# The constants' load moved behind the first loads of a_re and a_im

## The chip, the cores and the metric

The kernel runs on one core of a Trainium2 chip. The core has five engines that work side by side, each through its own list of instructions in order: PE (TensorE, matrix products), ACT (ScalarE, functions), DVE (VectorE), POOL (GpSimd) and SP (SyncE, which here only issues transfers). Sixteen DMA engines move the data; SP and ACT can both issue transfers, each through a queue of its own, and both queues are worked off by the same sixteen engines. The metric is the device time of one execution in microseconds (us), the median of several runs.

## The reference, cut to what matters

A gated linear recurrence with complex gates over 4 batches, 8 heads, 768 positions and 48 channels, followed by a feed-forward block over the 3072 rows of its output:

```
mag = sqrt(a_re^2 + a_im^2); scale = min(mag, 0.999) / (mag + 1e-6)
a = (a_re + i a_im) * scale
for t in range(768):  S = a[t] * S + outer(k[t], v[t]);  y[t] = q[t] @ real(S)
h = y @ w_in;  solu = h * softmax(h);  ln = layernorm(solu) * g_ln;  out = ln @ w_out
```

The kernel does not step through t. It takes the logarithm of the gates' size and their angle, sums both along a chunk of 128 positions by a product with a triangular matrix of ones on PE, and turns the sums back into factors on q and k. With these, a chunk is a masked product of q and k, times v, plus what the state carries over. So nothing of a chunk can reach PE before a_re and a_im of that chunk have gone through ACT and DVE, and PE's first product needs the triangular matrix, one of the constants.

## The kernel before

The work is cut into 6 stretches of 128 positions times 4 batches, 24 chunks in all. Two chunks (a pair of batches) form a group: 12 groups share the loads and the preparation of the gates. The feed-forward block follows chunk by chunk. The weights arrive as 64-bit numbers and are converted on the core in 7 pieces during the first groups.

The order on every engine is written out by hand: the string `ORDER` (from L516) names some 1,200 steps as `name:index`, and the loop at the end of `whole` calls them in that order. Each step appends its instructions to the lists of the engines that it uses, SP's included, so the order in `ORDER` is also the order of the issues of transfers. A name without a step, as `init:0`, does nothing.

The first steps, in the order of the string: `load_aia`, `load_ara`, `load_arb`, `load_aib` (`load_one`, L702 to L707) load a_im and a_re of group 0, half by half, 192 KB each; only group 0 is loaded and prepared in halves, a and b. `inverse` (L823) has ACT take the logarithm of a_re (L824, f_lr) and its reciprocal (L825, f_x). `ratio` has DVE multiply a_im by it (L830) and a_re by it (L831). Then come `sure`, `tangent`, `square`, `secant`, `size`, `eps`, `lnm`, alternating between ACT and DVE, until f_lr holds the logarithm of the gates' size. `total` (L881) multiplies it by the triangular matrix on PE into f_L: the first work of PE, 8 products for each half. `decay` and `grow` take the exponentials, `last` sends the last row to f_rows (L900), `turn_ends` reads f_rows on PE into f_tot.

Between these, SP issues further loads: `load_q`, `fetch:5` and `fetch:1` (a piece of w_out as two transfers, and a piece of w_in, into f_raw, L746), `load_v`, `load_k`, `fetch:0` (a piece of w_in into f_w_mix), and, behind `last`, a_im and a_re of group 1, further weight pieces and `load_vr` (L715, f_vr: four transfers of v in another row order, read with f_v by the product f_y, L1087). `up` (L1128) is the feed-forward block's first product, f_h.

The constants f_mats are five matrices of 128 x 128 (unit matrix, triangular matrices, ones), 320 KB, kept as data of the program. One transfer brings them in, issued by ACT ahead of its first step:

```
1279  to_exp()
1280  nc.scalar.dma_start(out=mats, in_=nc.inline_tensor(fast_constants(), ...
```

`to_exp` loads ACT's table of logarithm and exponential. f_mats is read by PE in `total`, and later in `phase`, the transposes and the masks.

The transfers issued by SP and ACT together use eight completion semaphores. Each transfer is given one of them when the program is built, and SP waits before each issue until the last transfer with the same semaphore has landed. In the program before, f_mats has the third place in this count, behind the first halves of a_im and a_re; f_q has the sixth.

Of the kernel before, what the change touches and what calls it, by code (L numbers as in the profile page):

```python
# [516 lines left out]
init:0 load_aia:0 load_ara:0 inversea:0 load_arb:0 ratioa:0 load_aib:0 surea:0 load_q:0 tangenta:0 fetch:5 fetch:1  # L517
inverseb:0 squarea:0 ratiob:0 secanta:0 sureb:0 sizea:0 load_v:0 tangentb:0 epsa:0 load_k:0 lnma:0 squareb:0 secantb:0
fourthb:0 sizeb:0 total0:0 epsb:0 fourtha:0 raised:5 lnmb:0 decay0:0 grow0:0 total1:0 grow1:0 decay1:0 fetch:0 trig:0
anglea:0 convert:5 phase0:0 last:0 raised:1 qs0:0 angleb:0 convert:1 phase1:0 nearest0:0 part0:0 turn_ends:0  # L520
nearest1:0 ks0:0 ks1:0 sina:0 cosa:0 load_ai:1 qs1:0 part1:0 q2:0 tot:0 sinb:0 k2:0 cosb:0 exp:0 qt1:0 load_ar:1 qT1:0
raised:0 q2:1 kt1:0 k2:1 convert:0 kT1:0 inverse:1 ratio:1 kt0:0 qt0:0 qT0:0 kT0:0 fetch:2 score1:0 fetch:6 qt0:1
qT0:1 load_vr:0 score0:0 qt1:1 sure:1 raised:2 load_q:1 mask0:0 values:0 tangent:1 kt1:1 fetch:3 square:1 secant:1
turned_x:0 convert:2 qT1:1 up0:0 fetch:4 raised:6 size:1 eps:1 convert:6 lnm:1 fourth:1 onward:0 up1:0 gain:0 total1:1
load_k:1 kT1:1 raised:3 exp0:0 grow1:1 total0:1 decay0:1 grow0:1 carry:1 convert:3 solu0:0 decay1:1 trig:1 angle:1
kt0:1 phase1:1 ks1:1 qs0:1 kT0:1 add:1 phase0:1 ks0:1 score1:1 raised:4 nearest0:1 score0:1 nearest1:1 convert:4
part0:1 carry:0 part1:1 mean:0 mean:3 mean:7 add:0 sin:1 cos:1 mask0:1 load_q:2 q2:2 k2:2 mean:1 zt0:0 exp:1 load_ar:2
mean:4 mean:2 inverse:2 values:1 mean:5 kqb:2 turned_x:1 load_ai:2 ratio:2 mean:6 zT0:0 meansum:0 again:5 last:1
centre:3 centre:7 up1:1 sure:2 tangent:2 load_v:1 kqt0:2 square:2 zt1:0 centre:1 centre:2 secant:2 centre:0 centre:4
size:2 centre:6 eps:2 centre:5 up0:1 k2:3 turn_ends:1 qs1:1 score1:2 lnm:2 onward:1 centred:0 load_vr:1 score0:2 tot:1  # L530
down0:0 total0:2 zT1:0 total1:2 load_k:2 q2:3 exp0:1 fourth:2 mask0:2 down1:0 solu0:1 decay0:2 grow0:2 grow1:2
load_ar:3 decay1:2 kqb:3 trig:2 mixed:1 zt0:1 kqt0:3 last:2 values:2 angle:2 spread:0 zT0:1 on:2 phase1:2 ks1:2 norm:0
qs0:2 turned_x:2 phase0:2 carry:2 load_ai:3 nearest1:2 nearest0:2 up0:2 part1:2 part0:2 sin:2 add:2 cos:2 ks0:2 k2:4
q2:4 centred:1 exp:2 zt1:1 zT1:1 inverse:3 scale:0 up1:2 kqb:4 score1:3 score0:3 down0:1 mask0:3 ratio:3 exp0:2
turn_ends:2 spread:1 sure:3 solu0:2 load_q:3 values:3 tangent:3 load_v:2 down1:1 square:3 tot:2 turned_x:3 secant:3
size:3 load_k:3 carry:3 qs1:2 up0:3 kqt0:4 eps:3 norm:1 up1:3 k2:5 onward:2 zt1:2 lnm:3 lh:3 zt0:2 exp0:3 q2:5 scale:1
zT0:2 zT1:2 fourth:3 score1:4 ll:3 score0:4 mixed:0 total0:3 load_vr:2 total1:3 down0:2 kqb:5 down1:2 solu0:3 decay0:3
grow0:3 grow1:3 decay1:3 mask0:4 add:3 centred:2 trig:3 blocks:3 values:4 angle:3 on:3 xh:3 kqt0:5 store:1 store:0
spread:2 xl:3 last:3 phase1:3 turned_x:4 phase0:3 ks0:3 ks1:3 qs0:3 nearest0:3 score1:5 load_ar:4 centred:3 score0:5
nearest1:3 carry:4 load_ai:4 norm:2 part0:3 up0:4 part1:3 sin:3 cos:3 up1:4 mask0:5 turn_ends:3 exp:3 add:4 scale:2  # L540
k2:6 q2:6 away:3 inverse:4 values:5 exp0:4 kqb:6 ratio:4 down0:3 load_q:4 solu0:4 spread:3 turned_x:5 sure:4 load_v:3
tangent:4 qs1:3 down1:3 carry:5 kqt0:6 square:4 blocks:4 secant:4 size:4 onward:3 up0:5 away:4 eps:4 k2:7 norm:3 up1:5
q2:7 lnm:4 lh:4 tot:3 fourth:4 score1:6 ll:4 score0:6 exp0:5 total0:4 load_vr:3 load_k:4 kqb:7 total1:4 kqt0:7 solu0:5
scale:3 decay0:4 grow0:4 grow1:4 decay1:4 mask0:6 add:5 down0:4 trig:4 down1:4 centred:5 values:6 angle:4 on:4 xh:4
centred:4 qs0:4 xl:4 spread:4 last:4 store:2 phase1:4 turned_x:6 phase0:4 ks1:4 nearest0:4 ks0:4 nearest1:4 blocks:5
score1:7 carry:6 load_ai:5 part0:4 load_ar:5 part1:4 norm:4 score0:7 up0:6 sin:4 add:6 turn_ends:4 cos:4 exp:4 scale:4
away:5 store:3 inverse:5 mask0:7 up1:6 k2:8 q2:8 kqb:8 values:7 spread:5 exp0:6 ratio:5 down0:5 sure:5 load_q:5
solu0:6 turned_x:7 load_v:4 tangent:5 down1:5 square:5 qs1:4 kqt0:8 blocks:6 secant:5 onward:4 carry:7 up0:7 norm:5
size:5 eps:5 q2:9 k2:9 away:6 load_vr:4 lnm:5 up1:7 load_k:5 lh:5 fourth:5 scale:5 exp0:7 score1:8 ll:5 score0:8
total0:5 tot:4 kqb:9 total1:5 down0:6 kqt0:9 solu0:7 grow1:5 decay1:5 mask0:8 decay0:5 grow0:5 trig:5 down1:6 add:7  # L550
centred:7 blocks:7 values:8 angle:5 on:5 inspect:5 xh:5 centred:6 xl:5 spread:6 phase1:5 last:5 qs0:5 store:4
turned_x:8 phase0:5 ks1:5 load_ar:6 nearest1:5 nearest0:5 ks0:5 carry:8 load_ai:6 score0:9 score1:9 part1:5 part0:5
mask0:9 up1:8 sin:5 norm:6 up0:8 cos:5 add:8 turn_ends:5 scale:6 exp:5 inverse:6 store:5 k2:10 q2:10 values:9 kqb:10
ratio:6 exp0:8 solu0:8 away:7 turned_x:9 onward:5 down0:7 load_q:6 sure:6 down1:7 load_v:5 spread:7 tangent:6 square:6
blocks:8 qs1:5 kqt0:10 carry:9 secant:6 fourth:6 up0:9 norm:7 size:6 k2:11 away:8 eps:6 lnm:6 tot:5 load_vr:5 up1:9
q2:11 lh:6 scale:7 exp0:9 load_k:6 score0:10 score1:10 ll:6 total0:6 kqb:11 total1:6 down0:8 kqt0:11 solu0:9 grow1:6
decay1:6 mask0:10 decay0:6 grow0:6 trig:6 down1:8 add:9 centred:9 blocks:9 angle:6 values:10 on:6 xh:6 centred:8
store:6 xl:6 qs0:6 spread:8 last:6 phase1:6 turned_x:10 phase0:6 nearest0:6 ks1:6 nearest1:6 score1:11 carry:10
load_ai:7 score0:11 ks0:6 load_ar:7 away:9 part0:6 part1:6 cos:6 up0:10 sin:6 norm:8 mask0:11 up1:10 turn_ends:6
scale:8 exp:6 add:10 inverse:7 spread:9 store:7 values:11 k2:12 q2:12 kqb:12 ratio:7 exp0:10 down0:9 onward:6 solu0:10  # L560
load_q:7 turned_x:11 sure:7 down1:9 tangent:7 qs1:6 carry:11 load_v:6 kqt0:12 square:7 blocks:10 up0:11 secant:7
size:7 norm:9 eps:7 k2:13 away:10 load_vr:6 scale:9 lnm:7 tot:6 up1:11 q2:13 lh:7 fourth:7 exp0:11 score1:12 load_k:7
ll:7 score0:12 total0:7 kqb:13 total1:7 down0:10 centred:10 kqt0:13 solu0:11 grow1:7 decay1:7 mask0:12 decay0:7
grow0:7 trig:7 down1:10 add:11 blocks:11 angle:7 values:12 on:7 xh:7 last:7 store:8 spread:10 centred:11 qs0:7 xl:7
ks0:7 phase1:7 turned_x:12 phase0:7 nearest1:7 ks1:7 nearest0:7 score0:13 score1:13 part1:7 part0:7 mask0:13 sin:7
load_ar:8 away:11 carry:12 load_ai:8 up0:12 cos:7 add:12 norm:10 turn_ends:7 scale:10 exp:7 store:9 up1:12 k2:14 q2:14
inverse:8 values:13 kqb:14 ratio:8 exp0:12 solu0:12 down0:11 load_q:8 turned_x:13 sure:8 down1:11 load_v:7 tangent:8
carry:13 qs1:7 spread:11 kqt0:14 square:8 blocks:12 secant:8 norm:11 size:8 onward:7 k2:15 tot:7 eps:8 away:12 lnm:8
load_vr:7 fourth:8 up0:13 lh:8 load_k:8 up1:13 q2:15 score1:14 score0:14 ll:8 scale:11 total0:8 kqb:15 total1:8
exp0:13 decay0:8 grow0:8 centred:12 mask0:14 grow1:8 decay1:8 down0:12 kqt0:15 solu0:13 trig:8 down1:12 add:13  # L570
centred:13 blocks:13 angle:8 values:14 on:8 xh:8 store:10 spread:12 xl:8 last:8 phase1:8 turned_x:14 phase0:8 ks0:8
score0:15 qs0:8 nearest0:8 score1:15 ks1:8 nearest1:8 part0:8 carry:14 load_ai:9 part1:8 sin:8 norm:12 mask0:15 cos:8
add:14 load_ar:9 up1:14 turn_ends:8 exp:8 up0:14 away:13 k2:16 q2:16 scale:12 inverse:9 store:11 values:15 kqb:16
ratio:9 exp0:14 spread:13 load_v:8 solu0:14 turned_x:15 sure:9 down0:13 load_q:9 down1:13 tangent:9 blocks:14 square:9
# [38 lines left out]
def whole(ctx, tc, flag, q, k, v, a_re, a_im, moe_w_in, moe_w_out, moe_g_ln, out):  # L613
# [663 lines left out]


    to_exp()
    nc.scalar.dma_start(out=mats, in_=nc.inline_tensor(fast_constants(), name="f_mats_np").ap().rearrange("p (n t) -> p n t", n=5))  # L1280
    nc.vector.memset(unit, 1.0)
    nc.vector.memset(quarter, -0.5 * math.pi)
    nc.vector.memset(small, math.log(1e-6))
# [90 lines left out]
```

## Time and profile before

| | |
|---|---|
| median of 3 runs | 415.65 us (415.19 to 415.83) |
| the profiled execution | 415.1 us, of which 413.1 are its span |
| granted clock of PE | 0.996 of full speed |
| DMA engines | 74.17 MB, 180 GB/s over the span; queue of SP 72.64 MB, queue of ACT 0.43 MB |
| f_ai, first half | issued 0.72, landing 3.9 us after |
| f_ar, first half | issued 1.23, landing 4.3 us after |
| f_mats | issued 0.75 by ACT, landing 3.1 us after |
| PE's first product (f_L) | 13.27 |

Times count from the start of the span. "SPq" and "ACTq" are issues of transfers; the time beside one is how long the engine stood in the issue, not how long the transfer took. What a transfer took is the time "to landing", from its issue to the moment its data are announced. The chain of waits is followed back from the last instruction of the run: each step is what released the next one, so that its early part says what the start of the run waited for. An engine that waits while another is busy costs nothing unless it stands in that chain.

### The profile page before, as it was taken

How to read it: one execution, taken by the hardware profiler on the slowest of the kernel's cores; microseconds unless marked ns; L12 is line 12 of the kernel's file. 1: busy time of each engine (PE TensorE's matmuls, PEld its weight loads, DVE VectorE, ACT ScalarE, POOL GpSimd, SP SyncE). 2: the span in 40 equal slices, each digit the busy share in tenths (PEclk: the TensorE clock that was granted, in tenths of full speed). 3: DMA queues.
4: the chain of work that ended last, by engine and by line, in shares of the span. 5: the costliest groups of instructions: out<-in, count | busy, mean ns of one | idle time of the engine just before them, and what ended most of it. 6: DMA issues, size and time to landing. Idle time of an engine off the chain costs nothing.

```text
span 413.1 us, 15874 instructions
## 1 busy us (share of the span) xinstructions
PE 379.1 (92%) x6968; PEld 202.7 (49%) x6968; DVE 337.0 (82%) x414; ACT 299.0 (72%) x487; POOL 64.5 (16%) x140
## 2 busy tenths in 40 slices
PE   0368779999999999999999999999999999999995
PEld 0025334455645554654554554555645656546543
DVE  3798999779799899898899889988988988855530
ACT  4997977977887777887877976877976967721332
POOL 3000000112112112112122112112112122101111
PEclk9999999999999999999999999999999999999998
DMA  9995947695877778877787877967759768797551
GB/s 216 286 280 153 222 101 171 159 211 128 207 165 170 167 177 180 182 157 167 179 175 165 207 163 160 206 157 172 163 138 215 158 155 206 232 208 187 171 216 49
DMA packets 167741, 74.17 MB, mean 180 GB/s; under 512 B 142576, under 2 KB 156016, under 8 KB 166896
## 3 DMA queue, kind: packets, MB, share of 16 engines
q1 hardware_dynamic: 167376, 72.64, 74.7%
q8 instruction: 57, 0.93, 0.9%
q10 hardware_dynamic: 288, 0.43, 0.4%
q14 instruction: 20, 0.16, 0.1%
HBM read 38.87 MB, written 4.72 MB: 106 GB/s over the span
## 4 chain that ended last, share of the span: by engine, by line
PE 81%; ACT 8%; DVE 5%; DMA 2%; issue 1%; SPq 1%; DVEq 0%; ACTq 0%
PE f_h L1128 28%; PE f_o L1193 27%; PE f_y L1087 9%; PE f_score L1054 7%; PE f_d L1095 3%; PE f_L L876 2%; PE f_phase L876 2%; DMA f_q<-in_q_dram 1%; DMA f_ar<-in_a_re_dram 1%; ACT f_cs L951 1%; PE f_y L1203 1%; PE f_o L1203 1%; ACT L986 1%; ACT L989 1%; DVE f_kb L1009 1%
## 5 line engine op out<-in xcount | busy, mean ns | idle before, releaser
L1128 PE MATMUL f_h<-f_w_in,f_xT 128*32 128x512 f32 x1152 | 131.4, 593 | 1.4 <-ACT f_xT L1121 1.2
L1193 PE MATMUL f_o<-f_w_mix,f_zT 128*32 128x384 f32 x1280 | 108.6, 487 | 0.0
L1128 PEld LDWEIGHTS f_h<-f_w_in,f_xT 128*32 128x32 f32 x1152 | 40.9, 110 | 66.4 <-issue 64.3
L1193 PEld LDWEIGHTS f_o<-f_w_mix,f_zT 128*32 128x32 f32 x1280 | 42.8, 110 | 54.1 <-issue 51.5
L1009 DVE STREAM_TRANSPOSE f_kb<-f_kq 128x1536 f32<-128x1536 f32 x22 | 56.5, 2570 | 1.4 <-DMA f_kqT<-f_kb 0.7
L1140 DVE SCALAR_TENSOR_TENSOR f_z<-f_h,f_z 128x1024 f32<-128x1024 f32 x24 | 29.1, 1213 | 13.5 <-ACT f_z L1136 13.5
L1180 POOL TENSOR_SCALAR f_s<-f_s,f_sum 128x1 f32<-128x1 f32 x24 | 11.7, 485 | 182.1 <-ACT f_z L1174 181.9
L1136 ACT ACTIVATE f_z<-f_h 128x1024 f32<-128x1024 f32 x24 | 24.4, 1018 | 21.0 <-PE f_h L1128 21.0
L1087 PE MATMUL f_y<-f_att,f_v 128*16 128x128 f32 (+1 forms) x384 | 36.7, 273 | 0.8 <-DVE f_att L1059 0.8
L1054 PEld LDWEIGHTS f_score<-f_kqT 96*32 96x32 f32 x1536 | 32.5, 112 | 10.0 <-issue 10.0
L1087 PE MATMUL f_y<-f_att,f_vr 128*32 128x128 f32 x384 | 36.8, 273 | 0.0
L1059 DVE TENSOR_TENSOR f_att<-f_score,f_mats 128x1024 f32<-128x1024 f32 x24 | 29.3, 1220 | 8.5 <-PE f_score L1054 8.4
L1054 PE MATMUL f_score<-f_kqT 96*32 96x64 f32 (+3 forms) x1536 | 34.0, 238 | 0.0
L1087 PE MATMUL f_y<-f_kqT,f_state 96*32 96x128 f32 (+1 forms) x640 | 33.2, 272 | 0.0
L1174 ACT ACTIVATE f_z<-f_z,f_less 128x1024 f32<-128x1024 f32 x24 | 27.3, 1138 | 0.0
L869 POOL TENSOR_TENSOR f_ll<-f_lr,f_lh 128x768 fp32r<-128x768 f32 x9 | 16.6, 1849 | 65.6 <-ACT f_lh L864 57.9
L1087 PEld LDWEIGHTS f_y<-f_att,f_v 128*32 128x32 f32 (+1 forms) x384 | 22.0, 103 | 7.5 <-issue 6.4
L1158 DVE STREAM_TRANSPOSE f_zb<-f_z 128x1024 f32<-128x1024 f32 x20 | 24.8, 1238 | 0.0
L1000 DVE TENSOR_TENSOR f_kq<-f_cs,f_k 128x768 f32<-128x768 f32 x24 | 22.9, 955 | 2.1 <-ACT f_cs L951 1.2
L1000 DVE TENSOR_TENSOR f_kq<-f_cs,f_q 128x768 f32<-128x768 f32 x24 | 22.9, 953 | 1.1 <-PE f_d L1095 0.5
L1087 PEld LDWEIGHTS f_y<-f_att,f_vr 128*32 128x32 f32 x384 | 22.3, 109 | 1.7 <-issue 1.7
L1171 POOL TENSOR_SCALAR f_less<-f_sum 128x1 f32<-128x1 f32 x24 | 6.3, 266 | 88.7 <-DVE f_z L1140 88.7
(124 smaller groups left out, 643.9 us busy)
## 6 DMA issues: line engine op xcount, KB each, us to landing
f_kqT<-f_kb SPq DMA_DIRECT2D x88, 192.0 KB, 3.3
f_zT<-f_zb SPq DMA_DIRECT2D x80, 128.0 KB, 3.1
f_raw<-in_moe_w_out_dram SPq DMA_DIRECT2D x14, 384.0 KB, 5.0
f_raw<-in_moe_w_in_dram SPq DMA_DIRECT2D x5, 1024.0 KB, 6.7
f_q<-in_q_dram SPq DMA_DIRECT2D x12, 384.0 KB, 4.9
f_v<-in_v_dram SPq DMA_DIRECT2D x12, 384.0 KB, 5.2
f_k<-in_k_dram SPq DMA_DIRECT2D x12, 384.0 KB, 3.9
out_dram<-f_ot SPq DMA_DIRECT2D x23, 192.0 KB, 3.6
```

What stands on the lines that cost most here:

```text
L869: nc.gpsimd.tensor_tensor(out=t, in0=st[src], in1=st[hi].bitcast(FP), op=OP.subtract)
L1000: nc.vector.tensor_tensor(out=t, in0=T["cs", g][:, i * H:(i + 1) * H], in1=heads(T[nm, g][:, i]).unsqueeze(2).to_broadcast([P, H, 2, D]), ...
L1009: nc.vector.transpose(out=t, in_=T["kq", c].rearrange("p n h (f j) -> p j (n h) f", j=3))
L1054: nc.tensor.matmul(out=scores[r0:r0 + 32, x, r:], lhsT=QK[:, r // 32, x], rhs=QK[:, r // 32:, H + x], start=True, stop=True)
L1059: nc.vector.tensor_tensor(out=st["att"].rearrange("p (i u) t -> p i u t", u=2), in0=scores.rearrange("p (i u) t -> p i u t", u=2), in1=mat ...
L1087: nc.tensor.matmul(**product)
L1128: nc.tensor.matmul(out=st["h"][r:r + 32, half * 512:(half + 1) * 512], lhsT=st["xT"][:, c * P + r:c * P + r + 32], rhs=w_in[:, c, half * 5 ...
L1136: nc.scalar.activation(out=z, in_=h, func=AF.Exp, accum_out=sums[:, n:n + 1])
L1140: nc.vector.scalar_tensor_tensor(out=st["z"], in0=st["h"], scalar=1.0, in1=st["z"], op0=OP.mult, op1=OP.mult, accum_out=st["sum"][:, 0:1])
L1158: nc.vector.transpose(out=st["zb"], in_=st["z"].rearrange("p (c s f) -> p s c f", s=4, f=32))
L1174: nc.scalar.activation(out=st["z"], in_=st["z"], func=AF.Square, bias=st["less"], accum_out=st["sum"][:, 1:2])
L1193: nc.tensor.matmul(out=st["o"][rows], lhsT=zT, rhs=w[:, c], start=(c == 0), stop=(c == KF - 1))
```

## The change

The constants' transfer is taken from ACT's queue and becomes a step of its own, issued by SP behind the four loads of a_re and a_im and ahead of `load_q`. The two first loads change places: a_re's first half is now the first transfer of all. All other steps stand in the same order on every engine. In the new program the places in the count of semaphores are a_re, a_im, a_re, a_im, f_mats; f_q stays the sixth, and all behind it are as before.

```diff
 ORDER = """
-init:0 load_aia:0 load_ara:0 inversea:0 load_arb:0 ratioa:0 load_aib:0 surea:0 load_q:0 tangenta:0 fetch:5 fetch:1
...
+init:0 load_ara:0 load_aia:0 inversea:0 load_arb:0 ratioa:0 load_aib:0 constants:0 surea:0 load_q:0 tangenta:0 fetch:5
...
     to_exp()
-    nc.scalar.dma_start(out=mats, in_=nc.inline_tensor(fast_constants(), name="f_mats_np").ap().rearrange("p (n t) -> p n t", n=5))
     nc.vector.memset(unit, 1.0)
...
-    steps["gain", 0] = gain
+    def constants():
+        nc.sync.dma_start(out=mats, in_=nc.inline_tensor(fast_constants(), name="f_mats_np").ap().rearrange("p (n t) -> p n t", n=5))
+
+    steps["gain", 0], steps["constants", 0] = gain, constants
```

The rest of `ORDER` is the same list, broken into lines at other places.

## The prediction

> **What bounds the kernel now.** I read the page first, then the chain of waits for the first 75 us, then the timeline of the first 28 us, then the windows of the stretches where the transfers run.
>
> ```profile
> PE 379.1 (92%) x6968; PEld 202.7 (49%) x6968; DVE 337.0 (82%) x414; ACT 299.0 (72%) x487; POOL 64.5 (16%) x140
> PE 81%; ACT 8%; DVE 5%; DMA 2%; issue 1%; SPq 1%; DVEq 0%; ACTq 0%
> ```
>
> These two lines of the page say that TensorE sets the pace of nearly the whole run: the chain lies on PE for 81% of the span, and from 92 to 400 us PE is busy 307.59 of 308 us. The change touches nothing there. It touches the 13 us before PE's first matmul; every later engine order is kept. So the question is how much earlier the chain can start, and whether anything after it stays at its old time. The start of the chain (columns: start us, us, what):
>
> ```profile
> 0.72 0.45 SPq L706
> 1.17 0.06 issue
> 1.23 4.33 DMA f_ar<-in_a_re_dram
> 5.56 0.02 issue
> 5.58 0.53 ACT f_lr L824
> 6.11 0.02 issue
> 6.13 0.53 ACT f_x L825
> 6.67 0.02 issue
> 6.69 0.57 DVE f_ai L830
> ```
>
> SP issues a_im's first half (0.72), then a_re's (1.23). a_re lands at 5.56, and only then does ScalarE start its logarithm, although its table was loaded at 2.00. From 5.58 on the chain goes through ACT and DVE without a transfer. So 3.6 us of ACT's idle time is this one landing. The timeline shows what shares the DMA engines with it:
>
> ```profile
> 0.72 0.45 SPq L706 DMA_DIRECT2D f_ai<-in_a_im_dram  x1
> 0.75 0.39 ACTq L1280 DMA_DIRECT2D f_mats<-f_mats_np  x1
> ...
> 8.71 6.24 SPq L698 DMA_DIRECT2D f_k<-in_k_dram  x1
> ...
> 13.27 1.50 PE L881 MATMUL f_L<-f_lr,f_mats 128*32 128x384 f32 x8 [13.27 <-DVE f_lr L859]
> ```
>
> f_mats (320 KB, landing 3.1 us after its issue, at 3.87) is not read before 13.27, yet it and a_im (192 KB, landing 3.9 us after 0.72, at 4.62) stand ahead of the 192 KB that the chain waits for.
>
> **a_re's first half goes first, the constants go last of the five.** The trace has no transfer that starts the kernel on an empty queue, so I bound its landing. The nearest rows are the lightly loaded transfers of the same 192-byte runs later on: f_vr (48 KB each) and f_k (384 KB), from 60 to 400 us:
>
> ```profile
> DMA to landing us min/median/max: 2.0/2.4/3.7
> ...
> DMA to landing us min/median/max: 3.6/3.8/6.7
> ```
>
> Between them lie 336 KB: 1.6 us by the minima, 1.4 us by the medians, so 4.8 or 4.2 ns a KB. For 192 KB this estimates 2.0 + 144 x 0.0048 = 2.7 us, or 2.4 + 144 x 0.0042 = 3.0 us. Issued at 0.72, a_re lands at 3.4 to 3.7; I take 3.57, since both rows are equally near. That is 5.56 - 3.57 = **1.99 us earlier**.
>
> Here the Trainium skill gives another figure. "DMA: Bandwidth & Descriptors", section on the anatomy of one DMA, fits a fixed 2.0 us plus bytes over 436 GB/s (for the GpSimd path): 2.45 us for 192 KB, so a landing at 3.17 and a gain of 2.39. The trace moved such short runs at 203 to 234 GB/s between 4.4 and 6.4 us, about half of that rate, so I keep 1.99 and let 2.4 be the upper end. The other end: a_re takes what a_im takes now as the first of the queue, 3.9 us beside the constants: landing 4.62, gain 0.94.
>
> *Who is late next.* DVE's L830 needs a_im's first half too. It is now second; both halves together are the 384 KB of an f_k, 3.6 to 3.8 us from 0.72, so 4.3 to 4.5. ACT delivers f_x at 3.57 + (6.69 - 5.56) = 4.70. ACT stays the later one, by 0.2 us at least, and L830 starts at 4.70 instead of 6.69. The second halves: a_re's is used by ACT at 8.49, then 6.50; by the same line 576 KB land at 5.3. a_im's is used at 9.58, then 7.59; 768 KB land at 6.1, and if SP issues it no sooner than today (3.65, landing 3.7 later) at 7.35, still in time. No transfer enters the chain of the first 13 us again.
>
> **The constants on SP's queue.** Their issue leaves ACT (0.39 us beside the table load, free: gain zero) and costs SP 0.4 to 0.8 us before f_q, by the issues around it (0.45 to 0.82). The 1088 KB of the five transfers land, by the line of the medians, at 0.72 + 2.4 + 1040 x 0.0042 = 7.5. PE reads them at 13.27 - 1.99 = 11.3. Margin 3.8 us. The skill has a rule that speaks against this edit: the section "Issuing engines are not separate DMA queues" says that a second issuing engine brings no bandwidth but saves the issuing engine's time, so giving the issue back to SP should cost up to 0.8 us of each later load. The row to weigh it by is f_k's issue above: SP stands 6.24 us in it, far above the 0.43 of the other issues, while the DMA engines work off what is queued. Those are the same bytes as before. By the rule alone f_q and all behind it come 0.8 us later; by the row SP merely stands that much shorter in f_k. I take zero, and carry 0.8 us into the margins below.
>
> **Semaphores.** Each issue of SP waits until the transfer eight places before it has landed. The five first transfers only change places among themselves, and f_q is sixth in both programs. Five later issues get a new predecessor (the w_in piece a_re's first half, f_v a_im's first, f_k a_re's second, f_w_mix a_im's second, the first f_rows the constants); these land by 7.5 at the latest, and only the w_in piece (7.76) and f_v (8.23) are issued before 8.7, behind landings before 5. Cost zero.
>
> **Does the gain survive?** It does if every later load still lands before its use, now 2 us earlier. Landings are issue plus us to landing; the use is the first reader in the timeline:
> - w_out piece: 13.0 at most (second issue 5.7, the longest of the three pieces 7.3), used 15.99, then 14.0.
> - w_in piece: 15.1 at most (7.76 + 7.3), used 19.12, then 17.1.
> - f_k: 18.1, used 23.22, then 21.2.
> - f_w_mix: 20.9, used 28.51, then 26.5.
> - second group's a_re: 25.5, used 30.03, then 28.0.
> - third weight piece (issue 21.76 + 8.4): 30.2, used 34.96, then 33.0.
> - f_vr (last of four, 27.2 + 6.7): 33.9, used 36.2, then 34.2.
>
> All hold at their old times, the last by 0.3 us only. Adding 0.8 us of delay breaks that one by 0.5. But it is not fixed at its old time: SP's issues behind f_rows (18.69) wait for the chain, which comes earlier, and the DMA engines have idle room to fill (columns: stretch and us, busy us of PE, PEld, DVE, ACT, POOL with counts, clock, DMA share, GB/s):
>
> ```profile
> 15.00:16.00 1.00, 0.00 (x0) 0.00 (x0) 0.39 (x1) 1.00 (x4) 0.00 (x0) 1.00 0.53 108
> ...
> 20.00:21.00 1.00, 0.45 (x4) 0.20 (x8) 1.00 (x1) 1.00 (x2) 0.00 (x0) 1.00 0.23 80
> ...
> 37.00:38.00 1.00, 0.91 (x17) 0.46 (x7) 0.96 (x2) 0.97 (x2) 0.00 (x0) 1.00 0.00 0
> ...
> 56.00:60.00 4.00, 2.15 (x41) 1.21 (x33) 3.96 (x4) 3.80 (x6) 0.00 (x0) 1.00 0.00 0
> ```
>
> At 20 to 21 us the DMA share is 0.23, so about 1 us of the 2 is passed on to the transfers behind it, and f_vr lands near 33. At 37 and at 56 us the DMA engines stand still: no backlog reaches past there, and all that is issued later is issued when the chain releases it. f_rows itself, now issued at 16.7, queues behind f_w_mix (SP is free at 16.45) and lands near 21; PE's f_tot wants it at 23.48 - 2.0 = 21.5, and the next work of PE starts 2.6 us behind that, which hides a delay up to there. From then on the program is the same one shifted. PE does not get faster; it starts sooner.
>
> **Sum.** 0 (issue on ACT) + 0 (issue on SP) + 0 (semaphores) - 1.99 (a_re's landing) = -1.99 us. The profiled run took 415.1 us (span 413.1 and 2.0 around it), which becomes 413.1; its 415.1 is 0.55 under the median. On the median: 415.65 - 1.99 = **413.66 us**, 0.48% less. About 0.2% (0.83 us) can be told from no change.
>
> **Rivals.**
> - *Less is won at the head* (0.14): a first transfer has a start of its own, or the four run into one another and a_re lands with a_im. For it: a_im as first took 3.9 us. Against it: 320 KB of constants ran beside it. Gain 0.94 at the worst bound, 414.7 us.
> - *The middle takes it back* (0.10): the transfers between 15 and 34 us stay at their old times or come 0.8 us later, and PE waits for f_vr in f_y. For it: DMA shares of 0.9 to 1.5 from 22 to 32 us. Against it: the gaps at 15 and 20 us. With all 0.8 us and no earlier landing, f_y starts at 34.7 instead of 34.2: 0.5 us lost, 414.2. For no change the landing would have to move to 36, which no row suggests (0.01).
> - *The constants land too late* (0.05, the slower side): they are last of five and PE's first product needs them. The two sets of 8 products take 1.50 us each, and the second starts at 16.22 now. A landing after 12.7 begins to cost (16.22 - 1.99 - 1.50), after 14.7 the kernel is slower than before; at 16.0 it is 1.3 us slower, 416.9. For it: f_k took 9.4 us to land, in a crowded queue. Against it: 14.7 needs over 10 us for 320 KB that only 768 KB precede.
> - *The change does not do what it says* (0.04): the transfers start in order but the landings do not follow, a_re arrives at 5.6 as before. 415.6.
>
> **How the numbers follow.** My forecast has 0.67. Faster by over 0.2%: the forecast, most of the first rival (0.10 of its 0.14) and 0.09 of the second, 0.86. Within 0.2%: the rest of these and most of the fourth, 0.09. Slower: 0.05. The range runs from 412.9 (gain 2.4, and 0.4 for the scatter of medians, seen as 415.19 to 415.83) to 415.0 (gain 0.94 and 0.3 of scatter); it leaves out the slower case and no change.
>
> **What would show it.** Right: ACT's first L824 at about 3.6, L830 at 4.7, PE's first f_L at 11.3, the first f_h near 37.1 instead of 39.1, and the same 2 us at every later PE step. Wrong: L830 waiting for f_ai's DMA; f_L waiting for f_mats; f_y's first product waiting for f_vr at 34; or a shift that is 2 us at 12 and less at 40.

## The result, and the profile after

| | before | after |
|---|---|---|
| median | 415.86 us (414.40 to 417.46, 20 runs) | 414.42 us (413.44 to 415.26, 20 runs) |
| ratio after to before | | 0.9960, 95% interval 0.9947 to 0.9972 |
| profiled execution (span) | 415.1 us (413.1) | 413.44 us (411.5) |
| granted clock of PE | 0.996 | 1.000 |

The ratio makes it 0.40% faster: 1.66 us of 415.86, with an interval from 1.16 to 2.20 us. The two medians differ by 1.44 us, which lies in it. That the two profiled executions differ by 1.66 us as well is chance: single executions of one program scatter by more than 1 us.

The two lines of the page of the program after that answer to those of before:

```profile
PE 379.8 (92%) x6968; PEld 206.9 (50%) x6968; DVE 337.0 (82%) x414; ACT 298.7 (73%) x487; POOL 64.3 (16%) x140
PE 84%; ACT 8%; DVE 5%; issue 2%; DMA 1%; DVEq 0%; ACTq 0%
```

No engine does less: PE is busy for 379.8 us instead of 379.1, DVE for 337.0 in both. What left the chain is waiting on transfers: DMA from 2% to 1%, SPq from 1% to nothing. The start of the chain of waits of the program after (start us, us, what):

```profile
0.72 2.87 DMA f_ar<-in_a_re_dram
3.59 0.02 issue
3.61 0.53 ACT f_lr L825
4.14 0.02 issue
4.17 0.53 ACT f_x L826
4.70 0.02 issue
4.72 0.57 DVE f_ai L831
```

a_re's first half lands at 3.59 instead of 5.56, and the chain takes the same steps of the same length from there: 1.97 us earlier at each. The timeline of the program after shows the issues on SP and the first work of PE:

```profile
0.72 0.45 SPq L707 DMA_DIRECT2D f_ar<-in_a_re_dram  x1
...
3.44 0.99 SPq L1304 DMA_DIRECT2D f_mats<-f_mats_np  x1
8.77 6.38 SPq L699 DMA_DIRECT2D f_k<-in_k_dram  x1
11.31 1.50 PE L882 MATMUL f_L<-f_lr,f_mats 128*32 128x384 f32 x8 [11.31 <-DVE f_lr L860]
...
16.76 1.26 SPq L901 DMA_DIRECT2D f_rows<-f_ar  x2
...
21.64 0.45 PE L916 MATMUL f_tot<-f_mats,f_rows 16*32 16x16 f32 x6
```

The constants hold SP for 0.99 us, and SP still starts f_k's issue within 0.06 us of the old time. PE's first product starts when DVE has finished f_lr; the constants landed at 7.45, long before. The two stretches where the transfers had room before, in the windows of the program after (busy us of the engines with counts, clock, DMA share, GB/s):

```profile
15.00:16.00 1.00, 0.76 (x8) 0.00 (x0) 0.85 (x2) 0.84 (x3) 0.00 (x0) 1.00 0.39 81
...
20.00:21.00 1.00, 1.00 (x12) 0.20 (x8) 1.00 (x2) 0.58 (x1) 0.00 (x0) 1.00 0.97 320
```

At 20 to 21 us the DMA share rose from 0.23 to 0.97: the gap behind f_w_mix is filled. At 15 to 16 us it fell, from 0.53 to 0.39.

Up to 33 us all engines run 1.97 us ahead of before, and 1.92 us when f_h's first product starts (37.21, against 39.13). Then most of 0.5 us is lost at one place. First the timeline of DVE in the program before, then in the program after (line numbers are one higher there):

```profile
37.50 1.22 DVE L760 SCALAR_TENSOR_TENSOR f_w_in<-f_raw,f_w_in 128x1024 int32<-128x1024 int32 x1
38.86 1.23 DVE L762 CUSTOM_DVE_ANT_0 f_w_in<-f_w_in,f_bits 128x2048 uint16<-128x2048 uint16 x1
40.00 0.95 DVE L852 SCALAR_TENSOR_TENSOR f_lr<-f_u,f_lr 128x768 f32<-128x768 f32 x1
```

```profile
35.58 1.23 DVE L761 SCALAR_TENSOR_TENSOR f_w_in<-f_raw,f_w_in 128x1024 int32<-128x1024 int32 x1
36.70 0.46 ACT L1122 COPY f_xT<-f_y 128x384 f32<-128x384 f32 x1
37.38 1.23 DVE L763 CUSTOM_DVE_ANT_0 f_w_in<-f_w_in,f_bits 128x2048 uint16<-128x2048 uint16 x1 [0.57 <-ACT f_xT L1122]
```

Before, the two conversions follow each other: 37.50 + 1.22 = 38.72, next at 38.86. After, the first ends at 36.81 and the second starts at 37.38: DVE is idle for 0.57 us instead of 0.14. The releaser that the profile names, ACT's copy of f_xT, cannot be one: it ends at 37.16 and DVE does not read f_xT here. From there the gain is 1.48 us: 0.44 us went with this stall, 0.05 ahead of it. It stays at 1.4 to 1.5 us up to 230 us and is 1.1 to 1.4 us from there to the last 20 us. This stall is what the experiments are about.

### The profile page after: what moved, and what is told of

Its sections match the earlier page's. It is cut to its first block, busy times and chain, and to the rows that moved or that the text cites. A ratio compares the mean times of both kernels' runs of the same rounds, so it can differ in the third digit from the quotient of the medians.

```text
span 411.5 us, 15875 instructions
## 1 busy us (share of the span) xinstructions
PE 379.8 (92%) x6968; PEld 206.9 (50%) x6968; DVE 337.0 (82%) x414; ACT 298.7 (73%) x487; POOL 64.3 (16%) x140
## 3 DMA queue, kind: packets, MB, share of 16 engines
HBM read 38.87 MB, written 4.72 MB: 106 GB/s over the span
## 4 chain that ended last, share of the span: by engine, by line
PE 84%; ACT 8%; DVE 5%; issue 2%; DMA 1%; DVEq 0%; ACTq 0%
PE f_h L1129 29%; PE f_o L1194 27%; PE f_y L1088 9%; PE f_score L1055 7%; PE f_d L1096 3%; PE f_L L877 2%; PE f_phase L877 2%; PE f_L L882 1%; DMA f_ar<-in_a_re_dram 1%; PE f_zt L1149 1%; PE f_y L1204 1%; PE f_o L1204 1%; ACT L987 1%; ACT L990 1%; PE f_turned L1022 1%
## 5 line engine op out<-in xcount | busy, mean ns | idle before, releaser
L1194 PEld LDWEIGHTS f_o<-f_w_mix,f_zT 128*32 128x32 f32 x1280 | 45.7, 110 | 51.2 <-issue 46.3
L1137 ACT ACTIVATE f_z<-f_h 128x1024 f32<-128x1024 f32 x24 | 24.5, 1019 | 21.7 <-PE f_h L1129 21.6
L1088 PE MATMUL f_y<-f_att,f_v 128*32 128x128 f32 (+1 forms) x384 | 36.8, 273 | 0.7 <-DVE f_att L1060 0.7
L1060 DVE TENSOR_TENSOR f_att<-f_score,f_mats 128x1024 f32<-128x1024 f32 x24 | 29.2, 1218 | 8.6 <-PE f_score L1055 8.4
L1088 PEld LDWEIGHTS f_y<-f_kqT,f_state 96*32 96x32 f32 (+1 forms) x640 | 20.2, 106 | 0.0
```

The source lines that it names most:

```text
L1060: nc.vector.tensor_tensor(out=st["att"].rearrange("p (i u) t -> p i u t", u=2), in0=scores.rearrange("p (i u) t -> p i u t", u=2), in1=mat ...
L1088: nc.tensor.matmul(**product)
L1137: nc.scalar.activation(out=z, in_=h, func=AF.Exp, accum_out=sums[:, n:n + 1])
L1194: nc.tensor.matmul(out=st["o"][rows], lhsT=zT, rhs=w[:, c], start=(c == 0), stop=(c == KF - 1))
```

## The experiments

All ratios are to the program before on the same chip, with their 95% intervals. The program before had medians of 416.25, 416.08 and 416.02 us in the three groups of runs (e1 to e4, e5 to e8, e9 to e11).

**e1: the program after, unaltered.** Is the stall one execution's, or the program's?

> The changed kernel unaltered, once more. In its first profile the shift against before was 1.97 us from 5 to 37 us and 1.48 us behind DVE's L763 at 37.38, which stood 0.57 us with no releaser that fits. Theory A: this stall is an accident of one execution; the new profile has ACT's first logarithm at 3.6, PE's first product at 11.3, L763 at 36.9 without idle time, the shift stays near 2.0 to the end, and the median is 1.6 to 2.0 us under before. Theory B: the stall belongs to the new order; L763 starts at 37.4 again, and the gain stays at 1.4 to 1.5 us.

Median 414.38 us (12 runs), ratio 0.9967 (0.9951 to 0.9983). The stall is there again (0.58 us idle, L763 at 37.16), so it is the program's. All up to 33 us is as in the first trace (a_re's transfer 0.72 to 3.58, first f_L 11.30). In this execution PE's granted clock was 0.65 from 60 to 64 us, and at 75 us nothing of the gain was left in the trace. The last section returns to that; it is why what follows is read from places in the trace up to 40 us and from medians, not from the span of one execution.

**e2: the order of the two loads alone.** In the program before:

```diff
-init:0 load_aia:0 load_ara:0 inversea:0
+init:0 load_ara:0 load_aia:0 inversea:0
```

> The kernel before with a_re's first half ahead of a_im's; the constants still come first on ACT's queue. Theory A (the 2 us are made of two loads ahead of a_re, each worth about half): a_re lands as a_im did as the first of the queue beside the constants, 3.9 us behind 0.72, near 4.6; PE's first product near 12.3; gain about 1.0 us of the median. Rival (order alone does it, the constants' queue is no burden): landing near 3.6, gain as with the whole change, 1.5 to 2.0 us.

Median 415.01 us, ratio 0.9976 (0.9959 to 0.9992). The chain of waits of this kernel:

```profile
0.72 4.02 DMA f_ar<-in_a_re_dram
4.74 0.02 issue
4.77 0.53 ACT f_lr L824
```

a_re is alone on SP's queue when it starts, as in the program after, but the 320 KB of constants go on ACT's queue at the same time: 4.02 us instead of 2.87. DVE's first f_ai (L830) starts 0.81 us earlier than before. There is no stall at the second conversion (L762 at 38.12).

**e3: the constants alone.** In the program after the two loads are put back:

```diff
-init:0 load_ara:0 load_aia:0 inversea:0
+init:0 load_aia:0 load_ara:0 inversea:0
```

> The changed kernel with a_im's first half ahead of a_re's again; the constants stay behind the four loads on SP's queue. Theory A: a_re is second, issued at 1.23, and lands as a_im does in the changed kernel, 3.3 us behind its issue, near 4.5; PE's first product near 12.2; gain about 1.0 us. Rival (the constants alone did it): landing near 3.6 to 3.9, gain 1.7 us or more. Rival (the constants were harmless): landing near 5.5, no gain.

Median 415.58 us, ratio 0.9983 (0.9968 to 0.9999). The chain:

```profile
1.23 3.29 DMA f_ar<-in_a_re_dram
4.52 0.02 issue
4.54 0.53 ACT f_lr L825
```

f_ai (L831) starts 1.04 us earlier than before, and the stall of 0.58 us is there, in DVE's timeline:

```profile
38.33 1.22 DVE L763 CUSTOM_DVE_ANT_0 f_w_in<-f_w_in,f_bits 128x2048 uint16<-128x2048 uint16 x1 [0.58 <-ACT f_xT L1122]
```

So the stall comes with the constants' move, not with the order. At the head the halves are 0.81 and 1.04 us, 1.85 together against 1.97 for both at once: they add up but for 0.12 us. The cost of the stall falls on the constants' half.

**e4: the constants later still,** behind the first piece of w_in. In the program after:

```diff
-load_aib:0 constants:0 surea:0
+load_aib:0 surea:0
...
-fetch:1 inverseb:0
+fetch:1 constants:0 inverseb:0
```

> The changed kernel with the constants issued four transfers later, behind the first w_in piece. Theory: they land near 15 (14.5 to 16.8, by the bytes ahead of them), past the 12.7 from which PE's two sets of products are late; PE's second f_L starts 1.5 us behind the landing, near 16.5 instead of 14.26; the time is 1.7 to 2.5 us over the changed kernel, about that of before. Rival (PE's first products are not on the path at this point): no loss against the changed kernel.

Median 416.36 us (12 runs), ratio 1.0012 (0.9992 to 1.0033): 2 us over the program after, and no gain over before. The timeline of PE:

```profile
16.04 2.79 PE L882 MATMUL f_L<-f_lr,f_mats 128*32 128x384 f32 x16 [16.04 <-DMA f_mats<-f_mats_np]
```

Issued at 7.63, the constants land at 15.90, and PE's first product waits for that DMA. PE makes up a part, since both sets of 8 products then run together (2.79 us instead of 1.50 twice, with a gap); from 21.6 us on the kernel is 1.06 us behind before, and the stall at L763 adds 0.44. This is the slower rival of the prediction, made real. With this landing it is slower at 21.6 us in the trace; in the medians it is level with before. The place of the constants behind the four loads, not later, is what makes the change safe.

**e5: the program after with one DVE instruction more.** I read the instruction lists of both programs. Moving the constants to SP changes which transfer semaphores have been waited for when DVE comes to its first mask (L1060): after, DVE has a wait of its own there for the constants, and before it has none. In the trace of before the constants carry the same semaphore as f_k, for which DVE has waited long before the mask; in that of after they share one with f_rows, for which DVE has no wait ahead of the mask. All later places in DVE's list move by one:

```
place in DVE's list     before                   after
59                      L1059 (first mask)       wait for the constants
60                      L839                     L1060 (first mask)
61                      L758                     L840
62                      L760 (1.22 us)           L759
63                      wait for L760's end      L761 (1.23 us)
64                      L762 (1.23 us)           wait for L761's end
65                      L852                     L763 (1.23 us)
```

The traces show the same order with every place one lower; it seems that one entry at the head of the list has no record there. The differences between programs are measured, the count of 64 rests on the list.

So L763 is the 65th entry instead of the 64th, with a wait as the 64th. If the program came in blocks and one ended at 64, a 1.23-us instruction at that place would cover the fetching of the next, and a wait would not. One instruction more, early and without use, would then take the stall away:

```diff
     nc.vector.memset(unit, 1.0)
+    nc.vector.memset(unit, 1.0)
```

> The changed kernel with one more DVE instruction: the first memset is written twice. In four programs out of four with the constants on SP's queue DVE stood 0.57 us before L763 (the third use of that line, convert:2), in none of the two with the constants on ACT's queue. DVE waits for the constants' landing only in the former, by one instruction of its own ahead of the first L1060, so that all later DVE instructions stand one place further on; L763 is the 65th instead of the 64th. Theory A (a place in DVE's instruction list at which the next block of instructions has to come in; it costs 0.57 us when a wait stands last in the old block, and nothing when a long operation does): with one more instruction the wait itself becomes the 65th, the block comes in while L761 runs for 1.23 us, L763 starts without idle time, and the shift against before stays near 1.97 us past 40 us. Theory B (the wait for something that the constants' move has made late): the stall stays 0.57 us.

Median 413.70 us (12 runs), ratio 0.9955 (0.9936 to 0.9974). DVE's timeline:

```profile
35.53 1.22 DVE L761 SCALAR_TENSOR_TENSOR f_w_in<-f_raw,f_w_in 128x1024 int32<-128x1024 int32 x1
36.89 1.23 DVE L763 CUSTOM_DVE_ANT_0 f_w_in<-f_w_in,f_bits 128x2048 uint16<-128x2048 uint16 x1
```

The stall is gone: L763, now the 66th with L761 as the 64th, starts 0.14 us after L761's end instead of 0.57, with an instruction more to do.

**e6: the same instruction added to the program before.** No transfer moves here.

> The kernel before with one more DVE instruction, the first memset written twice. Theory A: L762 becomes the 65th instruction of DVE, with its wait as the 64th, and stands 0.57 us, as L763 does in the changed kernel; everything behind it comes about 0.45 us later than in before, though no transfer was moved. Theory B: no stall there, L762 starts right behind L760.

Median 416.69 us, ratio 1.0021 (1.0000 to 1.0041). DVE's timeline:

```profile
37.59 1.22 DVE L760 SCALAR_TENSOR_TENSOR f_w_in<-f_raw,f_w_in 128x1024 int32<-128x1024 int32 x1
39.39 1.23 DVE L762 CUSTOM_DVE_ANT_0 f_w_in<-f_w_in,f_bits 128x2048 uint16<-128x2048 uint16 x1 [0.57 <-ACT f_xT L1121]
```

L762 is now the 65th behind a wait, and the stall of 0.57 us appears, down to the same false releaser: 0.53 us later than before, 0.09 of it already at L760. It needs neither the new queue nor the new order, only the place.

**e7 and e8: more load on SP.** How much margin has the middle, which the prediction gave as 0.3 us for the last transfer? One transfer of weights into columns of f_w_out that are written again later is added on SP between the constants and f_q; 384 KB in e7, twice that in e8 (`w_out[:, 0:4]`):

```diff
+    def ballast():
+        nc.sync.dma_start(out=w_out[:, 2:4]..., in_=moe_w_in...)
...
-load_aib:0 constants:0 surea:0
+load_aib:0 constants:0 ballast:0 surea:0
```

> The changed kernel with one transfer more of 384 KB on SP's queue between the constants and f_q (into a part of f_w_out that is overwritten later). It delays all loads behind it by 1.2 us, at the 330 GB/s that the windows show for such rows, and adds one issue to SP. Theory A (these loads are covered): nothing behind it becomes late, since the w_in piece has 1.4 us left and f_vr 2.3 us; same time as the changed kernel within 0.3 us. Rival (each SP issue or each byte ahead of f_q is paid): 0.5 to 1.2 us slower than the changed kernel.

> The same with 768 KB, so about 2.4 us of delay for all loads behind the constants. Theory A (the cover is used up): the w_in piece, landing at 15.8 at the latest in the changed kernel, lands near 18.2 where DVE wants it at 17.16; SP issues f_rows near 19 instead of 16.76; 0.5 to 1.5 us slower than the changed kernel, about as much of it at the w_in piece as at f_vr. Rival (fully covered): same time as the changed kernel.

e7: median 413.86 us, ratio 0.9960 (0.9938 to 0.9981). e8: 415.14 us, ratio 0.9989 (0.9969 to 1.0010). The issue of f_rows in the timeline and the wait for it, e7 and then e8:

```profile
17.82 1.27 SPq L901 DMA_DIRECT2D f_rows<-f_ar  x2
PE f_tot L916 <- DMA f_rows<-f_ar: 1.8, 1, 1.8
```

```profile
17.95 1.27 SPq L901 DMA_DIRECT2D f_rows<-f_ar  x2
PE f_tot L916 <- DMA f_rows<-f_ar: 2.1, 1, 2.1
```

The first to be late is f_rows, which f_tot waits for, and not the w_in piece that I had named. f_rows is issued 1.06 us later in e7 and 1.19 us in e8. PE's first f_turned is still on time (24.37 and 24.42, against 24.41 after), so PE's gap behind f_tot covers most of it; the second waits longer for ACT, and PE's next f_turned, at 28.20 after, starts at 28.41 and 28.67. At f_h's first product 0.2 us of this is left in e7 (37.41) and 0.3 in e8 (37.52). f_y is later by as much, but waits for DVE's masks and not for f_vr. The ballast also moves the places of the transfers in the count of semaphores, and DVE's wait ahead of L1060 is gone again: L763 is 64th in both, and neither has the stall (L763 at 37.15 and 37.26). So e7's level result is two things that cancel, 0.2 us lost at f_rows and 0.4 won at L763. In e8's trace the sum is 0.1 us in its favour as well, and its span is 411.8; that its median lies 1.3 us over e7's does not show in its trace, and stays open.

**e9, e10, e11: a better version, and a test from the other side.** If the place decides, one instruction fewer must do what one more does. In the program after:

```diff
-    nc.vector.memset(unit, 1.0)
+    nc.gpsimd.memset(unit, 1.0)
```

e10 is e5 again and e11 the program after again, run beside it.

> The program after, with the one-column fill of 1.0 done by GpSimd instead of DVE: DVE has one instruction less, so L763 is its 64th again, as L762 was in the program before. No transfer moves and DVE loses work, not gains it. Theory A (the 0.57 us stall hangs on the place in DVE's list): no stall at L763, which starts near 36.9 instead of 37.4; the same from a minus as from a plus of one. Median 0.5 us under the program after. Theory C (the added fill helped by delaying DVE's start, or by something else that an instruction more brings): the stall of 0.57 us is there, L763 near 37.4, median as the program after.

> The program after with the second fill on DVE, once more, beside the program after on one chip. Theory A: no stall at L763 (36.9), and a median 0.5 us under that of the program after run beside it; with 20 runs each the intervals should still touch. Rival: the difference of 0.7 us between the medians seen before was scatter, and the two are within 0.2 us.

> The program after, unaltered, as the measure for the two others: stall of 0.57 us at L763 again near 37.4, ratio to the program before 0.996 to 0.997.

| | median us | runs | ratio to before |
|---|---|---|---|
| e9, one fewer | 413.71 (412.96 to 414.29) | 6 | 0.9947 (0.9931 to 0.9963) |
| e10, one more | 414.43 (412.26 to 415.01) | 8 | 0.9955 (0.9937 to 0.9972) |
| e11, after | 414.48 (413.20 to 415.76) | 12 | 0.9963 (0.9947 to 0.9978) |

DVE's timeline in e9, then in e11:

```profile
35.70 1.23 DVE L761 SCALAR_TENSOR_TENSOR f_w_in<-f_raw,f_w_in 128x1024 int32<-128x1024 int32 x1
37.06 1.22 DVE L763 CUSTOM_DVE_ANT_0 f_w_in<-f_w_in,f_bits 128x2048 uint16<-128x2048 uint16 x1
```

```profile
35.29 1.23 DVE L761 SCALAR_TENSOR_TENSOR f_w_in<-f_raw,f_w_in 128x1024 int32<-128x1024 int32 x1
37.09 1.22 DVE L763 CUSTOM_DVE_ANT_0 f_w_in<-f_w_in,f_bits 128x2048 uint16<-128x2048 uint16 x1 [0.57 <-ACT f_xT L1122]
```

One fewer removes the stall as one more did (in e10 L763 starts at 36.48, 0.15 us after L761's end). The medians of one group don't settle the worth: e10 is level with e11, e9 is 0.8 us under it. Over all runs, the 26 without the stall (e5, e9, e10) have a mean of 413.89 us and the 44 of the program after (the result, e1, e11) 414.49, with standard errors of 0.14 and 0.10: 0.61 us, with an interval of about 0.26 to 0.95 that the 0.44 of the traces lies in. These groups ran on more than one chip; e9, e10 and e11, on the same one, give 0.64 us with an interval of 0.01 to 1.27. The program after with its fill on GpSimd has the lowest ratio, from 6 runs only; it can't be told from e5 and e10.

**e12: the same place, 64 entries later.** Is there such a place at every 64? In the program after:

```diff
-    nc.vector.memset(unit, 1.0)
+    for _ in range(65):
+        nc.vector.memset(unit, 1.0)
```

> The program after with 64 fills more at the head of DVE's list (0.03 us each, 1.9 us in all, done by about 4.2, ahead of f_ai at 4.72, so the head keeps its time). The wait for L761's end is then the 128th entry of DVE's list and L763 the 129th. Theory A1 (the stall comes at every place 64 n + 1 that follows a wait): stall of 0.57 us at L763, near 37.4. Theory A2 (only at this place of the list, or in longer steps than 64): no stall, L763 near 36.9. If a block of the program is fetched at the stall, the packet of the instruction queue should come between L761's end and L763's start; in the trace of before with one fill more it came 0.05 us behind L763's start, which speaks against it.

The head did not keep its time: each of these fills waits for the one before, since all write the same column, so 65 take 8.06 us and not 1.9, f_L starts 5.37 us later, and the one execution took 417.86 us against 415.05 of one of the program before. The place can be read all the same. DVE's timeline:

```profile
40.66 1.23 DVE L761 SCALAR_TENSOR_TENSOR f_w_in<-f_raw,f_w_in 128x1024 int32<-128x1024 int32 x1
42.03 1.23 DVE L763 CUSTOM_DVE_ANT_0 f_w_in<-f_w_in,f_bits 128x2048 uint16<-128x2048 uint16 x1
```

L763 is the 129th entry behind a wait at 128, and starts 0.14 us after L761's end: no stall. So not every step of 64 entries has it. The trace of e12 holds a second answer: the fills run over the places around 65 of the list. They start 0.125 us apart from the first to the last, without one late step, though a fill of 0.06 us could cover nothing. So place 65 costs nothing by itself either, and the theory that I tested by e5 is too simple.

## Why the prediction was right, and where it was not

The direction and the range held; the forecast of 1.99 us was 0.33 too much against the ratio's 1.66, and lies in its interval. So do the 1.48 us that the trace leaves behind the stall: the run times alone can't tell the two apart, the traces can.

- **a_re's landing** was put at 3.57 and came at 3.59. The two later rows of the same 192-byte runs, f_vr and f_k, were good neighbours: a_im's first half came at 4.50 (4.3 to 4.5 was said), the constants at 7.45 (7.5). That a_re came within 0.02 us is luck, since 3.57 was the middle of 3.4 to 3.7. The fit of the Trainium skill ("DMA: Bandwidth & Descriptors", section on the anatomy of one DMA), which I had weighed against them, gives an estimate of 2.45 us for the transfer; it took 2.87 here and 2.86 in e1. The measurement decides for the rows.
- **Who is late next** at the head: L831 at 4.72 (4.70 was said), first f_L 11.31 (11.3), f_h 37.21 (37.1). a_im and the second halves were nowhere waited for.
- **The constants on SP's queue**: they were in time, and e4 shows what it costs if not. The issue took 0.99 us, over the 0.4 to 0.8 that I gave, and was swallowed in f_k's issue as said: SP was free at 16.65, I had 16.45. What the Trainium skill says in "DMA: Bandwidth & Descriptors", section "Issuing engines are not separate DMA queues", that a second issuing engine saves time of issuing, made no loss of this size here: of 0.99 us more on SP, 0.2 was left behind f_k.
- **Semaphores, "Cost zero"**: right for the waits of SP, which is what I counted. The step looked at one engine too few. The same count of places decides which engines need a wait for a transfer, and DVE got one more. This wait costs nothing where it stands, since DVE then waits for f_score anyway.
- **The gain's survival** failed at the sentence "From then on the program is the same one shifted". It is the same list of work on each engine, but not the same list of instructions: DVE's is one longer from place 59 on, and 0.44 of the 1.97 us won went where the conversion is the 65th entry. e5, e6 and e9 show that the place decides. The added wait can be read from the two instruction lists before a run; the stall behind it could not.
- **The margins in the middle** held, and were ordered wrongly. One reading was off: the second w_out issue of before starts at 7.28 and not at 5.7 (the timeline merges it with the first), but it lands 4.3 us later, at 11.6, under the 13.0 that I gave. The last f_vr was issued at 26.1 and landed 6.0 later, at 32.1, against the 33 of the prediction and a need at 34.4; I had called it the tightest. The tightest is f_rows for f_tot, by e7 and e8. I had it land near 21; in the program after its two transfers took 4.3 us each (2.2 before) and landed at 21.5 and 21.75, and f_tot started at 21.64, 0.13 us later than the shift alone. That still cost nothing. I took the 2.6 us behind it as full cover; in e7 a wait of 1.8 us cost 0.2.
- **Rivals.** "Less is won at the head" and "does nothing" fell with the landing at 3.59. "The middle takes it back" named the right stretch of the run and the wrong cause: no transfer was late. "Constants too late" fell, and e4 bounds it.

**How far the cause of the stall is settled.** Shown: it is there in the four programs in which this conversion is the 65th entry of DVE's list behind a wait (after, in three executions, e3, e4 and e6), and in none of the seven in which it is the 64th (before, e2, e7, e8, e9), the 66th (e5, twice) or the 129th (e12). Adding the constants' wait ahead of it is what put it there. Not shown: that DVE then stands because a block of its program is fetched. The traces have packets of 8 KB on the queue that the page lists as "q14 instruction", and they speak against the plain form of it. One comes at 36.97 in the program after, 0.16 us behind L761's end and 0.41 ahead of L763. But in thirteen of the fourteen traces a packet comes 0.1 to 0.4 us behind this end, with the stall and without (38.89 before, 36.91 in e5, 42.07 in e12), and in e6, which has the stall, it comes only behind the start of the stalled instruction (39.45 against 39.39). So it does not follow DVE's place. Another packet does: it comes at 39.26 in the program after (1.9 us behind the stalled start), at 32.26 and 33.45 with one instruction more (e5, e10), and at 8.64 in e12, when DVE stands at place 66 and no fill is late. Near place 129 e12 has only the first of the two packets, where all the others have both, so it does not test whether the stall comes back in longer steps. What DVE does in this 0.57 us stays open.

## What to carry to other kernels

At the head of a kernel, put the transfer that the chain waits for first on an empty queue, and issue what is needed late behind it on the same queue, not beside it on another: here each of the two was worth about a microsecond. Bound it from below by a row of the same run length in the same trace. And compare the instruction lists of the two programs, waits included, before writing that the rest is "the same, shifted": an engine that stands idle between two of its own instructions, behind a releaser that it does not read, may stand there for its place in the list, and one instruction more or fewer ahead of it is a cheap test.

## What the runs showed of the hardware that was not expected

- DVE's idle time of 0.57 us that depends on the place of a wait and the operation behind it in its list, shown by e5, e6 and e9: taking an instruction away and adding one both remove it from the program after, and adding one puts it into the program before.
- A transfer of 192 KB that starts on an empty queue is slowed by 320 KB on another engine's queue: 4.02 against 2.87 us. Second on its queue behind 192 KB it took 3.29 (e3).
- PE's granted clock falls in single executions for a few microseconds. In the windows of e2:

```profile
49.00:50.00 1.00, 1.00 (x8) 0.37 (x12) 0.96 (x3) 1.00 (x2) 0.00 (x0) 0.50 1.19 239
...
51.00:52.00 1.00, 1.00 (x23) 0.55 (x19) 0.81 (x1) 0.16 (x1) 0.00 (x0) 0.50 0.99 316
```

The clock is 0.50 in both of these windows, and e2's 0.81 us of gain is lost there in this trace. In e5 0.74 us went the same way at 50 us, in e11 1.7 us by 64 us (clock 0.67 from 60 to 64); in these stretches of the first trace of the program after it did not occur. That is more than the stall, and one reason why a stall of half a microsecond needs some 25 runs of each side to show in the means. Whether a change can move it stays open.
- Fills of one column by DVE, each over the last, take 0.12 us each in e12 and 0.03 us when they go to different columns (starts at 0.80, 0.83 and 0.86 in the trace of the program after).
